# First four F chunks of a SwiGLU kernel with the pieces of D outermost, over eight PSUM banks

## The chip, the cores and the metric

The kernel runs on one core of a Trainium2 chip. Its engines work side by side: TensorE (PE, with its weight loads shown apart as PEld), VectorE (DVE), ScalarE (ACT), GpSimd (POOL) and SyncE (SP). SP and ACT here also issue the DMAs. The metric is the device time of one execution in microseconds (us), taken as the median of several runs. Before the change it is 163.83 us, from three runs between 163.23 and 163.96.

## The reference

The kernel computes a SwiGLU feed-forward layer in bfloat16:

```python
B, S, D, F = 1, 2048, 640, 1536

def reference(x, w_gate, w_up, w_down):
    g = _silu(x @ w_gate)
    u = x @ w_up
    return (g * u) @ w_down
```

## The kernel before

D = 640 is cut in five pieces of 128 rows (`KD`), F = 1536 in twelve chunks of 128 (`KF`), and the 2048 rows of x in four blocks of 512 (`S_BLK`, index `sb`). For a block and a chunk `fc`, `proj` (L189) multiplies the five pieces of one weight chunk into the transposed x and sums them in a PSUM bank: once with w_gate (`pg`), once with w_up (`pu`). `gate` (L204) lets ACT take the Silu of `pg` and DVE multiply it by `pu`; the product goes to `aT`. After twelve chunks, the block is multiplied by w_down (`po_t` at L256 for the last 128 columns, `po_a` at L285 for the first 512) and written out. DVE also computes the last four rows of the input by dot products (L144), a few after each gate of blocks 1 to 3.

Transposed x comes in two ways. Rows 0 to 255 are loaded as they are (`load_x`, one half on SP and one on ACT); TensorE transposes them (`transpose_chunk`, L177), and ACT copies pieces 0 and 1 and DVE pieces 2 to 4 from PSUM into `xT` (L187). All other rows come through transposing DMAs (`turn_x`, L109), rows 256 to 511 by the first of these.

The weights come in chunks of F, given by `W_CHUNKS` (L45). The first, F chunks 0 and 1, comes in four pieces, of which ACT issues pieces 0 to 1 of D of w_gate and 0 to 2 of w_up, and SP the rest (L113 to L116). Then SP issues the transposing load of rows 256 to 511, the later weight chunks in order (`load_w`, L82), and w_down (L122).

`head` (L213) writes out the order of the first stage by hand, and `keep_order` holds TensorE and ACT to it. Eighteen small matmuls on ones (`warm`, L173) run until x is there, then ten transposes, then five more of the small matmuls (`N_GAP`), and then the projections of F chunks 0 and 1: first for rows 0 to 255 (`late` is 256), chunk 0 of w_gate in two halves of 128 rows, and after that for rows 256 to 511, each chunk followed by its gate. The main loop starts at chunk 2 with matmuls 512 columns wide. DVE and SP are held to the order of the program to the end (L308, L309).

PSUM has eight banks here: four under the tag `gu` for `pg` and `pu`, two each under `po_a` and `po_b`, which serve the transposes and later the outputs.

Of the kernel before, what the change touches and what calls it, by code (L numbers as in the profile page):

```python
# [10 lines left out]
def _body(  # L11
# [8 lines left out]
    nc = tc.nc  # L20
    P = nc.NUM_PARTITIONS
    f32 = mybir.dt.float32
# [10 lines left out]
    KD = D // P  # L33
    KF = F // P
    S_BLK = 512
# [1 line left out]
    SUB = S_BLK // P  # L37
    DA = 512
    Q = 32
    N_WARM, N_GAP = 18, 5  # L40
    T = 4
    WT_STEP = 4
    PE_X = 2
    ROW_J = 0
    W_CHUNKS = [(0, 2), (2, 4), (4, 8), (8, 12)]  # L45
    assert D % P == 0 and F % P == 0 and S % S_BLK == 0 and D > DA and SUB == 4

    consts = ctx.enter_context(tc.tile_pool(name="consts", bufs=1))
# [2 lines left out]
    psum = ctx.enter_context(  # L51
        tc.tile_pool(name="psum", bufs=2, space=bass.MemoryType.PSUM)
    )
# [3 lines left out]
    xT = consts.tile([P, KD, S], bf16)  # L57
    wg_sb = consts.tile([P, KD, F], bf16)
    wu_sb = consts.tile([P, KD, F], bf16)
# [14 lines left out]
    wg_v = w_gate.rearrange("(kd p) f -> p kd f", p=P)  # L74
    wu_v = w_up.rearrange("(kd p) f -> p kd f", p=P)
    wd_v = w_down.rearrange("(kf p) d -> p kf d", p=P)

    def wslice(a, b):
        return slice(a * P, b * P)

    def load_w(eng, dst, src, a, b):
        eng.dma_start(out=dst[:, :, wslice(a, b)], in_=src[:, :, wslice(a, b)])  # L82

    def load_x(eng, c0, c1):
        eng.dma_start(out=x_sb[:, c0:c1, :], in_=x_v[:, c0:c1, :])  # L85
# [11 lines left out]
    def keep_order(engine):  # L97

        traced = [i for i in nc.cur_bb.bb.instructions if i.engine == engine]
        for a, b in zip(traced, traced[1:]):  # L100
            issue_order(a, b)
# [5 lines left out]
    def turn_x(c0, c1):  # L107
        s_sl = slice(c0 * P, c1 * P)
        nc.sync.dma_start_transpose(out=xT[:, :, s_sl], in_=xt_v[s_sl])  # L109

    load_x(nc.sync, 0, 1)
    load_x(nc.scalar, 1, 2)
    for dst, src, k in ((wg_sb, wg_v, 2), (wu_sb, wu_v, 3)):  # L113
        for eng, k0, k1 in ((nc.scalar, 0, k), (nc.sync, k, KD)):
            f_sl = wslice(*W_CHUNKS[0])
            eng.dma_start(out=dst[:, k0:k1, f_sl], in_=src[:, k0:k1, f_sl])  # L116
    turn_x(PE_X, SUB)
    nc.scalar.activation(silu_first[:], ones[:, 0:1], ACT.Silu)  # L118
    for a, b in W_CHUNKS[1:]:
        load_w(nc.sync, wg_sb, wg_v, a, b)  # L120
# [5 lines left out]
    def turn_w(dst, src):  # L126
        for a in range(0, KF, WT_STEP):
            nc.sync.dma_start_transpose(
                out=dst[:, a : a + WT_STEP, :], in_=src[:, a : a + WT_STEP, :]
            )  # L130
# [3 lines left out]
        out=x_row[:],  # L134
        in_=x2[S - T : S, :].rearrange("t d -> (t d)").partition_broadcast(P),
# [29 lines left out]
    def do_dots(n):  # L165
        for _ in range(n):
            next(dots, None)
# [3 lines left out]
    def warm(n):  # L171
        for _ in range(n):
            nc.tensor.matmul(  # L173
                pw[:, 0:P], lhsT=ones[:], rhs=ones[:], start=True, stop=True
            )

    def transpose_chunk(c, parts):  # L177
        c_sl = slice(c * P, (c + 1) * P)
        for copy, tag, k0, k1 in parts:
            pt = psum.tile([P, k1 - k0, P], bf16, tag=tag, name="pt")  # L180
            for kd in range(k0, k1):
                nc.tensor.transpose(  # L182
                    out=pt[:, kd - k0, :],
                    in_=x_sb[:, c, kd * P : (kd + 1) * P],
                    identity=ident[:],
                )
            copy(out=xT[:, k0:k1, c_sl], in_=pt[:])  # L187

    def proj(ps, w_sb, fc, sb, c0, c1):  # L189
        for kd in range(KD):  # L190
            nc.tensor.matmul(  # L191
                ps[:, c0:c1],
                lhsT=w_sb[:, kd, fc * P : (fc + 1) * P],
                rhs=xT[:, kd, sb * S_BLK + c0 : sb * S_BLK + c1],
                start=(kd == 0),
                stop=(kd == KD - 1),
            )

    def gu_tiles():
        pg = psum.tile([P, S_BLK], f32, tag="gu", name="pg", bufs=4)  # L200
        pu = psum.tile([P, S_BLK], f32, tag="gu", name="pu", bufs=4)
        return pg, pu

    def gate(pg, pu, sb, fc, n_s):  # L204

        s0 = sb * S_BLK
        sg = work.tile([P, S_BLK], f32, name="sg")
        nc.scalar.activation(sg[:, 0:n_s], pg[:, 0:n_s], ACT.Silu)  # L208
        nc.vector.tensor_tensor(  # L209
            out=aT[:, fc, s0 : s0 + n_s], in0=sg[:, 0:n_s], in1=pu[:, 0:n_s], op=ALU.mult  # L210
        )

    def head():  # L213

        dve, act = nc.vector.tensor_copy, nc.scalar.copy
        split = [(act, "po_a", 0, 2), (dve, "po_b", 2, KD)]  # L220
        late = PE_X * P
        (pg0, pu0), (pg1, pu1) = gu_tiles(), gu_tiles()
        warm(N_WARM)
        transpose_chunk(0, split)
        transpose_chunk(1, split)
        warm(N_GAP)
        proj(pg0, wg_sb, 0, 0, 0, P)
        proj(pg0, wg_sb, 0, 0, P, late)
        proj(pg1, wg_sb, 1, 0, 0, late)
        proj(pu0, wu_sb, 0, 0, 0, late)  # L230
        proj(pu1, wu_sb, 1, 0, 0, late)
        for fc, pg, pu in ((0, pg0, pu0), (1, pg1, pu1)):
            proj(pg, wg_sb, fc, 0, late, S_BLK)
            proj(pu, wu_sb, fc, 0, late, S_BLK)
            gate(pg, pu, 0, fc, S_BLK)
        keep_order(mybir.EngineType.PE)
        keep_order(mybir.EngineType.Activation)

    head()
    for sb in range(NSB):  # L240
        n_s = S_BLK if sb < NSB - 1 else S_BLK - T
        for fc in range(KF):
            if sb == 0 and fc < 2:
                continue
            pg, pu = gu_tiles()
            proj(pg, wg_sb, fc, sb, 0, n_s)
            proj(pu, wu_sb, fc, sb, 0, n_s)
            gate(pg, pu, sb, fc, n_s)
            if sb > 0 and fc < KF - 2:
                do_dots(2)  # L250


        n_t = (SUB if sb < NSB - 1 else SUB - 1) * P
        po_t = psum.tile([P, n_t], f32, tag="po_b", name="po_t")
        for kf in range(KF):
            nc.tensor.matmul(  # L256
                po_t[:],
                lhsT=wd_sb[:, kf, DA:D],
                rhs=aT[:, kf, sb * S_BLK : sb * S_BLK + n_t],
                start=(kf == 0),  # L260
                stop=(kf == KF - 1),
            )
        ot_t = outp.tile([P, n_t], bf16, name="ot_t")
        ot_q = outp.tile([P, n_t], bf16, name="ot_q")
        nc.scalar.copy(ot_t[:], po_t[:])  # L265
        do_dots(3)
        nc.vector.transpose(out=ot_q[:], in_=ot_t[:])  # L267
        for q in range(P // Q):
            nc.scalar.dma_start(
                out=out2[  # L270
                    sb * S_BLK : sb * S_BLK + n_t, DA + q * Q : DA + (q + 1) * Q
                ].rearrange("(i r) c -> r i c", r=Q),
                in_=ot_q[q * Q : (q + 1) * Q, :].rearrange("r (i c) -> r i c", c=Q),
            )

        for j in range(SUB):
            s0 = sb * S_BLK + j * P
            last = sb == NSB - 1 and j == SUB - 1
            cols = [(0, DA, "po_a")]
            if last:  # L280
                cols = [(0, DA // 2, "po_a"), (DA // 2, DA, "po_a"), (DA, D, "po_b")]
            for c0, c1, tag in cols:
                po = psum.tile([P, c1 - c0], f32, tag=tag, name="po_a")
                for kf in range(KF):
                    nc.tensor.matmul(  # L285
                        po[:],
                        lhsT=aT[:, kf, s0 : s0 + P],
                        rhs=wd_sb[:, kf, c0:c1],
                        start=(kf == 0),
                        stop=(kf == KF - 1),  # L290
                    )
                ot = outp.tile([P, c1 - c0], bf16, name="ot" if c1 < D else "ot_b")
                if c1 < D:
                    nc.scalar.copy(ot[:], po[:])  # L294
                    eng = nc.sync
                else:
                    nc.vector.tensor_copy(out=ot[:], in_=po[:])  # L297
                    eng = nc.scalar
                if 0 < j and not last:
                    do_dots(3)  # L300
                if sb == NSB - 1 and j == ROW_J:
                    row_tail()
                eng.dma_start(out=out2[s0 : s0 + P, c0:c1], in_=ot[:])
        if sb == 0:
            turn_x(2 * SUB, 3 * SUB)
            turn_w(wuT, wut_v)
            turn_x(3 * SUB, 4 * SUB)
# [107 lines left out]
```

## Time and profile before

| quantity | value |
|---|---|
| median of three runs | 163.83 us |
| the profiled execution | 163.65 us |
| its span, first to last instruction | 162.3 us |
| PE busy | 159.3 us (98%) |
| DVE busy | 110.9 us (68%) |
| ACT busy | 42.8 us (26%) |
| HBM read, written | 6.88 MB, 2.62 MB |

The profile is one execution. A line such as L191 is a line of the kernel's source, and where a helper holds the instruction, its line. In groups, `out<-in` are the program's names, followed by the shapes and the count; a figure in square brackets is the idle time of the engine before the instruction and what ended it. Matmuls overlap, so the busy times of several in a row are read from their starts. SPq and ACTq are the instruction queues that issue DMAs.

### The profile page before, as it was taken

The numbers are of one execution on the slowest core, as the hardware profiler recorded it, in microseconds if no ns is written. First come the engines' busy times: TensorE is split into PE (matmuls) and PEld (weight loads), VectorE is DVE, ScalarE is ACT, GpSimd is POOL, SyncE is SP. The second block draws the span as 40 slices with busy tenths as digits, with TensorE's granted clock in tenths as the row PEclk, the third lists the DMA queues.
The fourth block names the chain that finished last, engine by engine and source line by source line (L and its number), as shares of the span: only waits on it lengthen the run. The fifth ranks groups of instructions, "written<-read, shape, count | busy, mean of one in ns | idle before, by whom it ended". The sixth has DMA issues, their size and how long they took to land.

```text
span 162.3 us, 2114 instructions
## 1 busy us (share of the span) xinstructions
PE 159.3 (98%) x790; PEld 78.2 (48%) x802; DVE 110.9 (68%) x249; ACT 42.8 (26%) x74; POOL 0.6 (0%) x6
## 2 busy tenths in 40 slices
PE   9999999999999999999999999999999999999995
PEld 8854444444444444444444444444444444445454
DVE  2042233599469999979919999979964999993000
ACT  5032222112222222221222322221214222222121
POOL 1000000000000000000000000000000000000000
PEclk9999999999999999999999999999999999999999
DMA  7999999994179991003110000000320000000312
GB/s 215 261 341 348 362 215 232 226 227 88 43 180 175 227 221 38 4 0 34 65 65 0 4 0 2 0 0 1 64 69 32 0 0 0 0 0 4 50 39 73
DMA packets 42441, 15.86 MB, mean 98 GB/s; under 512 B 33216, under 2 KB 42304, under 8 KB 42432
## 3 DMA queue, kind: packets, MB, share of 16 engines
q1 hardware_dynamic: 33536, 14.72, 37.5%
q10 hardware_dynamic: 8896, 1.02, 4.0%
q8 instruction: 6, 0.10, 0.2%
q14 instruction: 3, 0.02, 0.1%
HBM read 6.88 MB, written 2.62 MB: 59 GB/s over the span
## 4 chain that ended last, share of the span: by engine, by line
PE 96%; DMA 2%; issue 1%; ACTq 0%; DVE 0%
PE pg L191 32%; PE pu L191 32%; PE po_a L285 26%; PE po_t L256 6%; DMA wg_sb<-in_w_gate_dram 2%; ACTq L85 0%; DVE ot_b L297 0%
## 5 line engine op out<-in xcount | busy, mean ns | idle before, releaser
L191 PE MATMUL pg<-xT,wg_sb 128*128 128x512 bf16 (+3 forms) x248 | 59.9, 370 | 0.5
L191 PE MATMUL pu<-xT,wu_sb 128*128 128x512 bf16 (+2 forms) x250 | 59.7, 370 | 0.0
L209 DVE TENSOR_TENSOR aT<-sg,pu 128x512 bf16<-128x512 f32 (+1 forms) x48 | 32.8, 683 | 32.9 <-PE pu L191 28.1
L208 ACT ACTIVATE sg<-pg 128x512 f32<-128x512 f32 (+1 forms) x48 | 28.6, 597 | 71.3 <-PE pg L191 68.1
L285 PE MATMUL po_a<-wd_sb,aT 128*128 128x512 bf16 (+2 forms) x212 | 42.4, 358 | 0.2
L144 DVE SCALAR_TENSOR_TENSOR prod<-wgT,x_row 128x640 f32<-128x640 bf16 x48 | 39.4, 821 | 1.1
L144 DVE SCALAR_TENSOR_TENSOR prod<-wuT,x_row 128x640 f32<-128x640 bf16 x48 | 39.4, 822 | 1.0
L191 PEld LDWEIGHTS <-wg_sb 128*128 128x128 bf16 x255 | 25.0, 100 | 27.3 <-DMA wg_sb<-in_w_gate_dram 0.4
L191 PEld LDWEIGHTS <-wu_sb 128*128 128x128 bf16 x250 | 24.5, 98 | 27.3
L285 PEld LDWEIGHTS <-aT 128*128 128x128 bf16 x216 | 20.7, 98 | 21.6
L294 ACT CAST ot<-po_a 128x512 bf16<-128x512 f32 (+1 forms) x17 | 9.5, 561 | 32.0 <-PE po_a L285 20.9
L256 PE MATMUL po_t<-aT,wd_sb 128*128 128x512 bf16 (+1 forms) x47 | 10.3, 365 | 0.1
L256 PEld LDWEIGHTS <-wd_sb 128*128 128x128 bf16 x48 | 4.7, 98 | 5.1
L297 DVE CAST ot_b<-po_a 128x128 bf16<-128x128 f32 x1 | 0.3, 293 | 9.9 <-PE po_a L285 9.9
L265 ACT CAST ot_t<-po_t 128x512 bf16<-128x512 f32 (+1 forms) x4 | 2.2, 559 | 11.6 <-PE po_t L256 11.6
L144 DVE DVE_READ_ACCUMULATOR prod<-wuT,x_row 128x1 f32 x48 | 4.0, 82 | 0.0
L144 DVE DVE_READ_ACCUMULATOR prod<-wgT,x_row 128x1 f32 x48 | 3.9, 82 | 0.0
L267 DVE STREAM_TRANSPOSE ot_q<-ot_t 128x512 bf16<-128x512 bf16 (+1 forms) x4 | 2.7, 679 | 1.7 <-ACT ot_t L265 1.7
L173 PE MATMUL pw<-ones 128*128 128x128 bf16 x23 | 2.8, 313 | 0.4 <-DVE ones L105 0.4
L187 DVE COPY xT<-pt 128x384 bf16<-128x384 bf16 x2 | 0.7, 358 | 3.1 <-PE pt L182 3.1
L173 PEld LDWEIGHTS <-ones 128*128 128x128 bf16 x23 | 2.4, 147 | 0.4 <-DVE ones L105 0.4
L118 ACT ACT_TABLE_LOAD x1 | 1.3, 1283 | 1.6 <-issue 1.6
(13 smaller groups left out, 4.6 us busy)
## 6 DMA issues: line engine op xcount, KB each, us to landing
wd_sb<-in_w_down_dram SPq DMA_DIRECT2D x1, 1920.0 KB, 14.5
out_dram<-ot SPq DMA_DIRECT2D x15, 128.0 KB, 1.7
wg_sb<-in_w_gate_dram SPq DMA_DIRECT2D x2, 640.0 KB, 7.8
wu_sb<-in_w_up_dram SPq DMA_DIRECT2D x2, 640.0 KB, 8.7
x_row<-in_x_dram SPq DMA_DIRECT2D x1, 640.0 KB, 5.0
out_dram<-ot_q ACTq DMA_DIRECT2D x12, 32.0 KB, 1.9
wg_sb<-in_w_gate_dram SPq DMA_DIRECT2D x1, 320.0 KB, 4.5
wu_sb<-in_w_up_dram SPq DMA_DIRECT2D x1, 320.0 KB, 5.0
```

The source lines that it names most:

```text
L118: nc.scalar.activation(silu_first[:], ones[:, 0:1], ACT.Silu)
L144: nc.vector.scalar_tensor_tensor(out=prod[:], in0=wT[:, fc, :], scalar=1.0, in1=x_row[:, t, :], op0=ALU.mult, op1=ALU.mult, accum_out=acc[ ...
L173: nc.tensor.matmul(pw[:, 0:P], lhsT=ones[:], rhs=ones[:], start=True, stop=True)
L187: copy(out=xT[:, k0:k1, c_sl], in_=pt[:])
L191: nc.tensor.matmul(ps[:, c0:c1], lhsT=w_sb[:, kd, fc * P : (fc + 1) * P], rhs=xT[:, kd, sb * S_BLK + c0 : sb * S_BLK + c1], start=(kd == 0 ...
L208: nc.scalar.activation(sg[:, 0:n_s], pg[:, 0:n_s], ACT.Silu)
L209: nc.vector.tensor_tensor(out=aT[:, fc, s0 : s0 + n_s], in0=sg[:, 0:n_s], in1=pu[:, 0:n_s], op=ALU.mult)
L256: nc.tensor.matmul(po_t[:], lhsT=wd_sb[:, kf, DA:D], rhs=aT[:, kf, sb * S_BLK : sb * S_BLK + n_t], start=(kf == 0), stop=(kf == KF - 1),)
L265: nc.scalar.copy(ot_t[:], po_t[:])
L267: nc.vector.transpose(out=ot_q[:], in_=ot_t[:])
L285: nc.tensor.matmul(po[:], lhsT=aT[:, kf, s0 : s0 + P], rhs=wd_sb[:, kf, c0:c1], start=(kf == 0), stop=(kf == KF - 1),)
L294: nc.scalar.copy(ot[:], po[:])
```

## The change

The first weight chunk now covers F chunks 0 to 3, and SP issues all of it in slices of D: w_gate as piece 0, pieces 1 to 2, pieces 3 to 4, then w_up as pieces 0 to 2 and 3 to 4. The transposing load of rows 256 to 511 is issued after these. For rows 0 to 255, the projections of all four chunks run together, with the piece of D as the outer loop and the chunk as the inner one, first all of w_gate and then all of w_up. Their eight sums stand in eight PSUM banks: `pg` in the four banks of `gu`, `pu` in those of `po_a` and `po_b`. Then rows 256 to 511 follow chunk by chunk, each with its gate, and the main loop starts at chunk 4. Of the five small matmuls ahead of the projections one stays.

```diff
-    N_WARM, N_GAP = 18, 5
+    N_WARM, N_GAP = 18, 1
...
-    W_CHUNKS = [(0, 2), (2, 4), (4, 8), (8, 12)]
+    W_CHUNKS = [(0, 4), (4, 8), (8, 12)]
+    N_EARLY = W_CHUNKS[0][1]
+    WG_KD = [(0, 1), (1, 3), (3, 5)]
+    WU_KD = [(0, 3), (3, 5)]
...
-    for dst, src, k in ((wg_sb, wg_v, 2), (wu_sb, wu_v, 3)):
-        for eng, k0, k1 in ((nc.scalar, 0, k), (nc.sync, k, KD)):
-            f_sl = wslice(*W_CHUNKS[0])
-            eng.dma_start(out=dst[:, k0:k1, f_sl], in_=src[:, k0:k1, f_sl])
+    f_sl = wslice(*W_CHUNKS[0])
+    for dst, src, parts in ((wg_sb, wg_v, WG_KD), (wu_sb, wu_v, WU_KD)):
+        for k0, k1 in parts:
+            nc.sync.dma_start(out=dst[:, k0:k1, f_sl], in_=src[:, k0:k1, f_sl])
     turn_x(PE_X, SUB)
...
-        (pg0, pu0), (pg1, pu1) = gu_tiles(), gu_tiles()
         warm(N_WARM)
         transpose_chunk(0, split)
         transpose_chunk(1, split)
         warm(N_GAP)
-        proj(pg0, wg_sb, 0, 0, 0, P)
-        proj(pg0, wg_sb, 0, 0, P, late)
-        proj(pg1, wg_sb, 1, 0, 0, late)
-        proj(pu0, wu_sb, 0, 0, 0, late)
-        proj(pu1, wu_sb, 1, 0, 0, late)
-        for fc, pg, pu in ((0, pg0, pu0), (1, pg1, pu1)):
-            proj(pg, wg_sb, fc, 0, late, S_BLK)
-            proj(pu, wu_sb, fc, 0, late, S_BLK)
-            gate(pg, pu, 0, fc, S_BLK)
+        pg = [
+            psum.tile([P, S_BLK], f32, tag="gu", name="pg", bufs=4)
+            for _ in range(N_EARLY)
+        ]
+        pu = [
+            psum.tile([P, S_BLK], f32, tag=tag, name="pu")
+            for tag in ("po_a", "po_b", "po_a", "po_b")
+        ]
+        for ps, w_sb in ((pg, wg_sb), (pu, wu_sb)):
+            for kd in range(KD):
+                for fc in range(N_EARLY):
+                    nc.tensor.matmul(
+                        ps[fc][:, 0:late],
+                        lhsT=w_sb[:, kd, wslice(fc, fc + 1)],
+                        rhs=xT[:, kd, 0:late],
+                        start=(kd == 0),
+                        stop=(kd == KD - 1),
+                    )
+        for fc in range(N_EARLY):
+            proj(pg[fc], wg_sb, fc, 0, late, S_BLK)
+            proj(pu[fc], wu_sb, fc, 0, late, S_BLK)
+            gate(pg[fc], pu[fc], 0, fc, S_BLK)
...
-            if sb == 0 and fc < 2:
+            if sb == 0 and fc < N_EARLY:
```

## The prediction

> **What bounds the kernel now.** I read the page first: its busy shares, its clock row and its chain. Columns of the first line are engine, busy us, share of the span and instructions.
>
> ```profile
> PE 159.3 (98%) x790; PEld 78.2 (48%) x802; DVE 110.9 (68%) x249; ACT 42.8 (26%) x74; POOL 0.6 (0%) x6
> ...
> PEclk9999999999999999999999999999999999999999
> ...
> PE 96%; DMA 2%; issue 1%; ACTq 0%; DVE 0%
> ```
>
> TensorE has work for 98% of the span, and 96% of the chain that ended last is TensorE. The 2% of DMA in the chain is one transfer, the first gate weights. From there to the end TensorE hardly stands still, so a microsecond won or lost in the head is one at the end, and nothing after the head needs costing if it is only shifted. The head is read in the timeline (start, length, engine, instruction, count, idle time before and its releaser).
>
> ```profile
> 2.48 0.98 PEld L182 LDWEIGHTS <-x_sb 128*128 128x128 bf16 x10 [0.26 <-DMA x_sb<-in_x_dram]
> 2.48 1.25 PE L182 MATMUL pt<-ident,x_sb 128*128 128x128 bf16 x10
> ...
> 2.96 0.86 ACT L187 COPY xT<-pt 128x256 bf16<-128x256 bf16 x2
> ...
> 3.52 0.74 PE L173 MATMUL pw<-ones 128*128 128x128 bf16 x5
> 3.77 0.36 DVE L187 COPY xT<-pt 128x384 bf16<-128x384 bf16 x1 [0.17 <-PE pt L182]
> ...
> 4.35 1.52 PEld L191 LDWEIGHTS <-wg_sb 128*128 128x128 bf16 x15 [0.36 <-DMA wg_sb<-in_w_gate_dram]
> 4.36 1.80 PE L191 MATMUL pg<-xT,wg_sb 128*128 128x128 bf16 x15
> ...
> 5.99 1.25 PE L191 MATMUL pu<-xT,wu_sb 128*128 128x256 bf16 x10
> ...
> 7.09 0.71 PE L191 MATMUL pg<-xT,wg_sb 128*128 128x256 bf16 x5
> ```
>
> The activations are turned by 4.13 (the DVE copy ends), the weights come at 4.35, and the projections start at 4.36. The other thing to see is the pace. Ten 256-wide matmuls take 5.99 to 7.09, so 109 ns each. The fifteen before take 4.36 to 5.99; five of them are 256 wide (0.55 us), so the ten 128-wide ones cost 1.08 us, 108 ns each: as much as matmuls twice as wide. Is that a floor of the weight load, or a slow clock? The clock row reads full speed all along, so I asked for the weight loads of 128-wide matmuls alone, in the head and in the kernel's last microsecond.
>
> ```profile
> 4.35 1.09 PEld L191 LDWEIGHTS <-wg_sb 128*128 128x128 bf16 x11 [0.36 <-DMA wg_sb<-in_w_gate_dram]
> ```
> ```profile
> 159.54 0.66 PEld L285 LDWEIGHTS <-aT 128*128 128x128 bf16 x11
> ```
>
> Eleven loads take 1.09 us in the head and 0.66 us at the end, about 100 against 56 ns a step. So until about 5.4 us TensorE runs at half pace, whatever the clock row says, and a 256-wide matmul there would take some 213 ns.
>
> **The sum's base.** The profiled execution took 163.65 us (span 162.3 and 1.35 around it), 0.18 below the median 163.83; three runs spread over 0.73.
>
> **First start of the projections.** Removed are ten weight DMAs (four pieces of chunk (0, 2), two on each queue, and six later chunk loads on SP); added are nine, all on SP (five slices of chunk (0, 4), four chunk loads). ACT keeps one of its three. The landings now:
>
> ```profile
> wg_sb<-in_w_gate_dram SPq DMA_DIRECT2D x1, 192.0 KB, 3.6
> wu_sb<-in_w_up_dram ACTq DMA_DIRECT2D x1, 192.0 KB, 4.5
> x_sb<-in_x_dram SPq DMA_DIRECT2D x1, 160.0 KB, 2.4
> x_sb<-in_x_dram ACTq DMA_DIRECT2D x1, 160.0 KB, 2.7
> wg_sb<-in_w_gate_dram ACTq DMA_DIRECT2D x1, 128.0 KB, 3.8
> ```
> ```profile
> 1.00:2.25 1.25, 1.25 (x14) 1.22 (x12) 0.00 (x0) 0.69 (x1) 0.00 (x0) 1.00 0.88 262
> 2.25:3.00 0.75, 0.75 (x9) 0.52 (x7) 0.00 (x0) 0.74 (x3) 0.00 (x0) 1.00 0.96 285
> ...
> 5.00:6.00 1.00, 1.00 (x12) 0.94 (x11) 0.00 (x0) 0.00 (x0) 0.00 (x0) 1.00 1.26 234
> 6.00:8.00 2.00, 2.00 (x21) 1.79 (x19) 0.00 (x0) 0.17 (x1) 0.00 (x0) 1.00 1.20 281
> 8.50:10.50 2.00, 1.95 (x14) 1.27 (x13) 1.34 (x2) 0.60 (x1) 0.00 (x0) 1.00 1.10 342
> ```
>
> (First list: KB, us from issue to landing. Second: stretch, busy us by engine, clock, DMA share, GB/s.) The first slice of w_gate is 128 KB behind 320 KB of x, 459 thousand bytes. At 262 and then 285 GB/s these have moved by 2.7 us. Landing trails movement by 0.6 us for x (328 thousand moved by 2.25, the second half landed at 0.13 + 2.7 = 2.8), by up to 1.0 for w_gate; so the slice lands between 3.3 and 3.7. The start then waits for the turned x instead. The first two pieces of D need ACT's copies alone; these end at 2.96 + 0.86 = 3.82. The last DVE copy starts 0.04 after the last transpose ends (2.48 + 1.25 = 3.73); with twice that, for a signal and a weight load, the start is 3.90. The third piece needs the DVE copy, 4.13, long before its turn. Gain in the start: 4.36 - 3.90 = 0.46 us; the bounds are 0 (slice as late as today) and 0.46 (the copies don't move). I take 0.46, since 3.7 lies below 3.9. The four dropped warm-ups (0.43 us at 107 ns) only filled this wait: the remaining one is through at 3.63, and TensorE stands for 0.27, against 0.30 now (4.06 to 4.36).
>
> **What 0.46 is worth.** In half pace it is 0.46/0.2135 = 2.15 wide matmuls, which at full pace would have cost 2.15 x 0.109 = 0.235 us. So -0.235, if the pace changes at 5.4 as before; the whole -0.46 if it changes before 3.9.
>
> **Merging the ten narrow matmuls of chunk 0** into five wide ones: 10 x 107 = 5 x 213 at half pace, 10 x 56 = 5 x 109 at full pace. Zero either way.
>
> **Chunks 2 and 3 in two halves.** Twenty 512-wide matmuls at 216 ns (1.08 us for five in the chain) become forty at 109: +0.05 us.
>
> **Eight banks, piece of D outermost.** Each matmul now writes another bank than the last. Today that happens every fifth matmul or so, as from pg to pu at 5.99 and back at 7.09, and the pace goes on at 109 ns. I take zero; a gain is excluded, since the pace has no gap to win. The bound above is the 0.07 us that 65 more changes would cost at 1 ns, the reading's grain.
>
> The Trainium skill ("TensorE: Matmul & The Clock Gate", section "A second HAM failure mode: psum-queue depth-cycling") speaks against this step: cycling through PSUM banks made TensorE idle for moments, and its clock fell back. By it the 72 matmuls after 5.4 us could stay at half pace, an estimate of 72 x 0.104 = 7.5 us, which the undisturbed bank changes in these rows don't bear out.
>
> **Will the data keep up on one queue?** Moved bytes go on from 2.7 us at 342 GB/s (1 KB rows on SP alone, the 8.50 row); landing 0.6 to 1.0 later. Wanted: start 3.90, 213 ns each to 5.4, then 109 ns. Slices 1-2 of w_gate: landed 4.1 to 4.5, wanted 4.75. Slices 3-4: 4.8 to 5.2, wanted 5.9. w_up 0-2: 6.0 to 6.4, wanted 6.8. w_up 3-4: 6.8 to 7.2, wanted 8.1. The transposing load of rows 256 to 511 is the step moved most: on SP it stands behind three issues more, of 0.41 to 0.49 us each, so at about 2.9 in place of 1.44, and its bytes stand behind 1.28 MB. At 234 GB/s (5.00 row) it has moved by 7.6 and lands at 8.2 to 8.6; wanted after 40 matmuls at 9.0. Chunk (4, 8) lands by 10.5 and 12.4, wanted 13.4 and 14.5. All covered, thinly for the transposing load. With the slices at 281 GB/s, the row of 512-byte rows, it lands at 8.9 to 9.3. SP's later issues and ACT's table load (1.56, now about 0.6) move ahead or stay; ACT's first copy waits for the transposes anyway.
>
> **PSUM after the head.** Chunk 4 takes the banks of pg 0 and 1, read by ACT some 3 us before; the last, pg 3, is read (0.60 us) 3 us before chunk 5's pu wants it. Four gates follow at 1.09 us each, DVE needs 0.69. Zero.
>
> Sum: 163.65 - 0.235 + 0.05 = 163.47, so 163.5.
>
> **Rivals.**
> 1. Narrow matmuls are bound by their weight loads. Then merging saves 10 x 107 - 5 x 109 = 0.53, the start its whole 0.46: 163.65 - 0.53 - 0.46 + 0.05 = 162.7. The 56 ns loads speak against it.
> 2. The first slice is no earlier (one landing trailed by 1.0 and might by more): 163.65 + 0.05 = 163.7.
> 3. The transposing load, or w_up, comes late. Slowest reading: all of it at 234 GB/s, so the load lands at 9.7 to 10.1 for 9.0; 0.9 of stall: 164.4.
> 4. Slower: half pace lasts longer. TensorE was busy from 0.39 to 5.4 with gaps of 0.2 and 0.3 before the pace changed. With only one warm-up as cover, a slice landing after about 3.9 makes the last gap longer than any seen. If that starts the 5.0 us anew from 3.9, full pace begins at 8.9: 3.5 us at half pace cost 3.5 x 0.49 = 1.7, so 163.47 + 1.7 = 165.2. For it: less cover than today. Against: the expected gap of 0.27 is below the 0.30 that did no harm.
>
> The Trainium skill (same page, section "Part 1: The HAM clock gate (the "warmup" mystery)") puts the change of pace at a free-running window of 3.4 us. That agrees with a change at 5.4 here; by it the moment would differ from run to run, and the sum would lie between 163.24 (change before 3.9) and 163.47.
>
> **How the numbers follow.** Forecast 0.52; rival 1 0.12, 2 0.15, 3 0.13, 4 0.08. The range reaches to rival 1 below and rival 3 above, 162.7 to 164.4, which leaves out rival 4 and little else. Under 0.5% (0.8 us) a measurement can hardly tell from no change, and forecast, 2 and 3 lie within it: faster is rival 1 and 0.05 of the forecast's own spread, 0.17; slower is rival 4 and the tail of 3, 0.11; same 0.72.
>
> **What would show it.** Right: the first pg matmul at about 3.9, its idle time put down to ACT's copy, 213 ns steps and then 109; no wait on w_up or the transposing load; chunk 4 at about 13.4 in place of 13.59, the rest shifted by as much. Wrong: a PE wait on a DMA around 6.8 or 9.0, steps of 213 ns past 5.5, or gate waits at chunk 4.

## The result and the profile after

The changed kernel takes 164.43 us (median of 22 runs, 163.63 to 165.69); the kernel before takes 163.68 in the same comparison (22 runs, 163.13 to 164.11). The ratio is 1.0051, with a 95% interval from 1.0032 to 1.0070: slower by half a per cent, 0.03 us above the predicted range and on the side that was given 0.11. Beside the higher median the spread has grown: five of the 22 runs lie above 165 us, none of before's above 164.2.

The profiled execution of the changed kernel is one of its quicker ones, 163.85 us (span 162.5). Its page:

```profile
PE 159.6 (98%) x813; PEld 79.1 (49%) x813; DVE 110.8 (68%) x249; ACT 42.8 (26%) x74; POOL 0.6 (0%) x6
...
PE 94%; DMA 3%; SPq 1%; DVE 0%; issue 0%
PE pg L194 30%; PE pu L194 30%; PE po_a L300 26%; PE po_t L271 6%; DMA wu_sb<-in_w_up_dram 3%; PE pu L240 1%; SPq L119 1%; SPq L88 0%; DVE ot_b L312 0%
```

For comparison, the last line as the kernel before has it:

```profile
PE pg L191 32%; PE pu L191 32%; PE po_a L285 26%; PE po_t L256 6%; DMA wg_sb<-in_w_gate_dram 2%; ACTq L85 0%; DVE ot_b L297 0%
```

TensorE is as busy as before. But the transfer in the chain is another one: not the first weights of w_gate, which started the projections before, but those of w_up, in their middle. The timeline of TensorE in the head (L240 are the early projections, L194 the rest):

```profile
3.38 0.31 PE L176 MATMUL pw<-ones 128*128 128x128 bf16 x1
3.73 1.01 PE L240 MATMUL pg<-xT,wg_sb 128*128 128x256 bf16 x4
5.14 1.92 PE L240 MATMUL pg<-xT,wg_sb 128*128 128x256 bf16 x16 [0.40 <-DMA wg_sb<-in_w_gate_dram]
7.22 2.36 PE L240 MATMUL pu<-xT,wu_sb 128*128 128x256 bf16 x20 [0.17 <-DMA wu_sb<-in_w_up_dram]
9.42 0.71 PE L194 MATMUL pg<-xT,wg_sb 128*128 128x256 bf16 x5
...
13.79 1.24 PE L194 MATMUL pg<-xT,wg_sb 128*128 128x512 bf16 x5
```

Chunk 4 of the kernel before:

```profile
13.59 1.24 PE L191 MATMUL pg<-xT,wg_sb 128*128 128x512 bf16 x5
```

The projections do start early, at 3.73. After four matmuls TensorE stands until 5.14 for the second slice of w_gate, runs sixteen at full pace, stands again until 7.22 for the first slice of w_up, and reaches chunk 4 at 13.79, where the kernel before is at 13.59. Those 0.2 us are the whole difference between the two profiled executions (163.85 and 163.65); from chunk 4 to the end both take the same.

The landings, as issues with KB and us from issue to landing, and the movement by stretch (last two columns: DMA share, GB/s):

```profile
wg_sb<-in_w_gate_dram SPq DMA_DIRECT2D x1, 128.0 KB, 2.6
wg_sb<-in_w_gate_dram SPq DMA_DIRECT2D x1, 256.0 KB, 4.2
...
wu_sb<-in_w_up_dram SPq DMA_DIRECT2D x1, 384.0 KB, 5.3
```
```profile
3.00:4.00 1.00, 0.97 (x9) 0.74 (x8) 0.72 (x2) 0.52 (x2) 0.00 (x0) 1.00 0.69 190
4.00:5.00 1.00, 0.74 (x4) 0.20 (x2) 0.00 (x0) 0.00 (x0) 0.00 (x0) 1.00 0.91 303
5.00:6.00 1.00, 0.86 (x8) 0.75 (x9) 0.00 (x0) 0.00 (x0) 0.00 (x0) 1.00 1.04 363
...
7.00:8.00 1.00, 0.83 (x9) 0.70 (x8) 0.00 (x0) 0.00 (x0) 0.00 (x0) 1.00 0.73 110
```

The row of the kernel before for 3 to 4 us:

```profile
3.00:4.00 1.00, 1.00 (x12) 1.00 (x10) 0.59 (x2) 0.69 (x3) 0.00 (x0) 1.00 1.07 313
```

From 3 to 4 us the DMA engines moved 190 GB/s where before moved 313, and the first slice of w_up, issued at 1.89, landed at 7.2. The trace has sixteen completion counts for each of these loads, and a load has landed with the last of them. For the second slice of w_gate fifteen came between 3.47 and 4.32 and the last at 5.09; for the first slice of w_up they came between 5.50 and 7.18.

### The profile page after: what moved, and what is told of

Its sections match the earlier page's. It is cut to its first block, busy times and chain, and to the rows that moved or that the text cites. A ratio compares the mean times of both kernels' runs of the same rounds, so it can differ in the third digit from the quotient of the medians.

```text
span 162.5 us, 2147 instructions
## 1 busy us (share of the span) xinstructions
PE 159.6 (98%) x813; PEld 79.1 (49%) x813; DVE 110.8 (68%) x249; ACT 42.8 (26%) x74; POOL 0.6 (0%) x6
## 4 chain that ended last, share of the span: by engine, by line
PE 94%; DMA 3%; SPq 1%; DVE 0%; issue 0%
PE pg L194 30%; PE pu L194 30%; PE po_a L300 26%; PE po_t L271 6%; DMA wu_sb<-in_w_up_dram 3%; PE pu L240 1%; SPq L119 1%; SPq L88 0%; DVE ot_b L312 0%
## 5 line engine op out<-in xcount | busy, mean ns | idle before, releaser
L194 PE MATMUL pg<-xT,wg_sb 128*128 128x512 bf16 (+2 forms) x240 | 57.4, 370 | 0.0
L194 PE MATMUL pu<-xT,wu_sb 128*128 128x512 bf16 (+2 forms) x240 | 57.4, 370 | 0.0
L194 PEld LDWEIGHTS <-wu_sb 128*128 128x128 bf16 x240 | 23.5, 98 | 26.1
L194 PEld LDWEIGHTS <-wg_sb 128*128 128x128 bf16 x240 | 23.5, 98 | 25.9
L240 PE MATMUL pg<-xT,wg_sb 128*128 128x256 bf16 x20 | 2.9, 300 | 0.4 <-DMA wg_sb<-in_w_gate_dram 0.4
L240 PEld LDWEIGHTS <-wg_sb 128*128 128x128 bf16 x20 | 2.0, 106 | 1.4 <-DMA wg_sb<-in_w_gate_dram 0.9
```

The lines of the kernel that those rows point to most:

```text
L194: nc.tensor.matmul(ps[:, c0:c1], lhsT=w_sb[:, kd, fc * P : (fc + 1) * P], rhs=xT[:, kd, sb * S_BLK + c0 : sb * S_BLK + c1], start=(kd == 0 ...
L240: nc.tensor.matmul(ps[fc][:, 0:late], lhsT=w_sb[:, kd, wslice(fc, fc + 1)], rhs=xT[:, kd, 0:late], start=(kd == 0), stop=(kd == KD - 1),)
```

## The experiments

Two theories stood at first. **L**: the slices land late and TensorE stands for them. **P**: with one small matmul in place of five, the gap ahead of the projections keeps TensorE at half pace for longer. All kernels were timed beside the kernel before on the same chip; its medians lay between 163.57 and 163.65. Where a short name is used below, it is that of the run.

### gap5: the small matmuls back

```diff
-    N_WARM, N_GAP = 18, 1
+    N_WARM, N_GAP = 18, 5
```

> The changed kernel with five small matmuls ahead of the projections again in place of one. Theory L (slices of the weights land late on one queue, and TensorE stands for them): the start moves from 3.73 to about 3.85, the wait in the middle shrinks by as much, and the end stays where the changed kernel has it, 164.3 to 164.6 us. Theory P (with one small matmul the gap ahead of the projections keeps the half pace longer): the cover is back, 163.4 to 163.7 us, and the spread falls to that of before.

Measured: 164.31 us (5 runs, 163.82 to 164.36), ratio 1.0036 [1.0023, 1.0049]. The projections start at 3.98, wait twice for w_gate, and the first matmul on w_up starts at 7.19, chunk 4 at 13.75. As L had it: cover ahead of the start changes nothing where the later slices decide.

### before_gap1: the small matmuls taken from the kernel before

```diff
-    N_WARM, N_GAP = 18, 5
+    N_WARM, N_GAP = 18, 1
```

> The kernel before with one small matmul ahead of the projections in place of five, nothing else. L: TensorE stands from 3.6 to 4.36 instead of 4.06 to 4.36 and ends as before, 163.5 to 163.8 us. P: the longer gap keeps the half pace in a part of the runs, 164.2 to 165 us with a wide spread.

Measured: 163.63 us (11 runs, 163.22 to 164.05), ratio 0.9995 [0.9982, 1.0009]. TensorE stood 0.67 us ahead of the projections, and the slowest run took 164.05. P in its first form is wrong: such a gap by itself costs nothing here. (In the profiled run the steps of TensorE fall from 106 to 55 ns at 3.3 us, so there the gap came after the change of pace.)

### twoq: two of the slices on ACT

```diff
-        for k0, k1 in parts:
-            nc.sync.dma_start(out=dst[:, k0:k1, f_sl], in_=src[:, k0:k1, f_sl])
+        for n, (k0, k1) in enumerate(parts):
+            eng = nc.scalar if n % 2 else nc.sync
+            eng.dma_start(out=dst[:, k0:k1, f_sl], in_=src[:, k0:k1, f_sl])
```

> The changed kernel with the second slice of w_gate and the second of w_up issued by ACT, the rest by SP. If L holds and the single queue is what delays the slices: the second slice lands before 4.6, no wait on a DMA after the start, 163.1 to 163.5 us. If L holds and the number of bytes delays them, whatever the queue: waits at the same places, 164.2 to 164.6. P: nothing changes for the gap, 164.4.

Measured: 164.23 us (6 runs, 164.18 to 165.22), ratio 1.0048 [1.0030, 1.0067]. The wait on w_gate is gone, that on w_up is longer:

```profile
4.03 2.93 PE L241 MATMUL pg<-xT,wg_sb 128*128 128x256 bf16 x20
7.93 2.36 PE L241 MATMUL pu<-xT,wu_sb 128*128 128x256 bf16 x20 [0.96 <-DMA wu_sb<-in_w_up_dram]
```

Two queues carried 350 GB/s from 3 to 4 us, and still w_up's first slice landed at 7.9; its second slice, on the other queue, now moved beside it. Spreading the slices over two queues does not take the wait on w_up away.

### narrow and narrow_defer: a quarter of the bytes, and a second limit

```diff
-    f_sl = wslice(*W_CHUNKS[0])
+    f_sl = wslice(0, 1)
...
-    for a, b in W_CHUNKS[1:]:
+    for a, b in [(1, 4)] + W_CHUNKS[1:]:
...
-                        lhsT=w_sb[:, kd, wslice(fc, fc + 1)],
+                        lhsT=w_sb[:, kd, wslice(0, 1)],
```

> The changed kernel with slices one F chunk wide (32 KB a piece of D, a quarter), which the early projections read for all four chunks; chunks 1 to 3 are loaded behind the transposing load. So rows 0 to 255 of chunks 1 to 3 are computed with the weights of chunk 0, and the output is another. Order, banks and small matmuls stay. L: no wait between the start at about 3.75 and the rows from 256 on, the main loop's chunk 4 at 13.0 to 13.4, 163.0 to 163.4 us. P: the gap ahead of the start is still there, 164.4 us and the wide spread.

Measured: 164.39 us (6 runs, 164.10 to 165.03), ratio 1.0050 [1.0035, 1.0065]. Half of L held: from 3.86 the forty early matmuls run without a wait. The gain is gone all the same. A first part is gone in the head: chunk 4 starts at 13.65, no earlier than before. The first twenty matmuls took 3.06 us, so with steps of 213 and 109 ns eight or nine of them ran at half pace, and TensorE waited 0.16 us at 10.75 for the weights of chunk 1, which this kernel loads late. The rest, 0.67 us, is lost later. These are DVE, ACT and TensorE between 33 and 40 us:

```profile
33.37 0.83 DVE L147 SCALAR_TENSOR_TENSOR prod<-wgT,x_row 128x640 f32<-128x640 bf16 x1 [1.50 <-DMA wgT<-in_w_gate_dram]
```
```profile
36.60 2.07 ACTq L284 DMA_DIRECT2D out_dram<-ot_q  x4
38.71 1.07 ACT L309 CAST ot<-po_a 128x512 bf16<-128x512 f32 x2 [4.42 <-DVE prod L147]
```
```profile
39.35 1.02 PE L300 MATMUL po_a<-wd_sb,aT 128*128 128x512 bf16 x4 [0.50 <-ACT ot L309]
```

The transposing load of w_gate for DVE's dot products comes late, DVE waits 1.50 us, three dot products stand ahead of the turn of 128 output columns (the kernel has such dot products in the output stage of every block, the first too, and not only after the gates), ACT issues the four stores of these columns ahead of its first output copy, and TensorE waits for the copy to free a PSUM bank. The stores and the first output copy, in the kernel before and in the changed kernel:

```profile
35.01 1.99 ACTq L269 DMA_DIRECT2D out_dram<-ot_q  x4
37.04 0.59 ACT L294 CAST ot<-po_a 128x512 bf16<-128x512 f32 x1 [2.81 <-DVE prod L144]
```
```profile
35.20 2.86 ACTq L284 DMA_DIRECT2D out_dram<-ot_q  x4
38.11 0.58 ACT L309 CAST ot<-po_a 128x512 bf16<-128x512 f32 x1 [3.68 <-DMA out_dram<-ot_q]
```

Before, that copy ended at 37.63, 1.0 us ahead of TensorE's need (38.62, two tiles of 2.59 us after 33.44). In the profile of the changed kernel it ended at 38.69, 0.13 us ahead of the need at 38.82: there ACT took 2.86 us over the four stores in place of 1.99, and DVE had not waited. So a second limit stands close behind the first (called D from here; what remains lost in the head is H), though in the profile of the changed kernel it cost nothing. Three runs here cut it, by moving the four stores of the first row block behind ACT's second output copy and holding ACT to that order.

```diff
+        def store_t():
...
+        if sb > 0:
+            store_t()
...
                 eng.dma_start(out=out2[s0 : s0 + P, c0:c1], in_=ot[:])
+            if sb == 0 and j == 1:
+                store_t()
...
```

> The kernel with slices of a quarter of the bytes, which the early projections read for all four chunks (so rows 0 to 255 of chunks 1 to 3 are computed with the weights of chunk 0), and with the four stores of the first row block behind the second output copy. With small slices no wait was left in the early projections, but the time stayed at 164.39, with a wait of 0.66 us at 38.5 us for the first output copy. If these are two separate limits: the wait at 38.5 is gone and the time falls to 163.5 to 163.8 us. If the lateness has another cause: 164.2 us or more.

Measured: 164.12 us (11 runs, 163.75 to 164.75), ratio 1.0030 [1.0013, 1.0047]. DVE waits the same 1.5 us for its load, ACT's first copy starts at 36.34 and the wait of TensorE at 38.5 is gone. But this execution waited 0.75 us at 10.2 for the weights of chunk 1. The profiles show the second limit in this kernel. The medians, 0.27 us apart with intervals that overlap, do not price it, and the time lay between the two expectations.

> The changed kernel, with the four stores of the turned 128 output columns of the first row block issued by ACT after its second output copy instead of ahead of the first. Theory H (all that is lost, is lost in the head, to waits on slices): 164.2 to 164.6 us as the changed kernel. Theory D (the head's loads push back the transposing load of w_gate, and through DVE's dot products, the turned columns and ACT's stores the first output copies come too late for TensorE at about 38.5 us): this path is cut, the copies wait for TensorE alone, 163.6 to 164.0 us, and the runs above 165 are gone.

Measured: 164.21 us (6 runs, 163.66 to 164.40), ratio 1.0046 [1.0030, 1.0062], no different from the changed kernel's 1.0051. So in the changed kernel most of the loss is H, as far as these intervals can tell. None of the six runs is above 165; with five of 22 before, that tells little.

> The kernel before with the same move of the four stores. In the profile of before the first output copy ends 1.0 us ahead of TensorE's need, so both H and D expect no difference: 163.5 to 163.8 us.

Measured: 163.59 us (12 runs), ratio 1.0002 [0.9985, 1.0019], as expected.

### gap18: start late

```diff
-    N_WARM, N_GAP = 18, 1
+    N_WARM, N_GAP = 18, 18
```

> The changed kernel with 18 small matmuls ahead of the projections in place of one, so these start some 1.5 us later, near 5.2. H: the waits in the projections are gone but for 0 to 0.3 us ahead of w_up, full pace from the start on, chunk 4 at 13.9 to 14.2, 163.9 to 164.3 us: the early start is worth nothing. D: TensorE reaches the first output copies later by 0.2 to 0.4 us, which hides part of the lateness there; the same times, and a smaller spread.

Measured: 164.22 us (6 runs, 164.06 to 164.66), ratio 1.0049 [1.0032, 1.0067]. In its profile the projections start at 4.86, 1.1 us after those of the changed kernel, and still wait, for slices that landed later in this execution:

```profile
4.86 1.47 PE L240 MATMUL pg<-xT,wg_sb 128*128 128x256 bf16 x12
6.75 1.05 PE L240 MATMUL pg<-xT,wg_sb 128*128 128x256 bf16 x8 [0.42 <-DMA wg_sb<-in_w_gate_dram]
8.00 2.36 PE L240 MATMUL pu<-xT,wu_sb 128*128 128x256 bf16 x20 [0.20 <-DMA wu_sb<-in_w_up_dram]
```

The start is worth nothing. With five profiles of the four-chunk order side by side, the rule of the head can be read off:

| kernel | first start | first w_up matmul | chunk 4 | profiled time |
|---|---|---|---|---|
| after_defer | 3.70 | 7.04 | 13.60 | 163.66 |
| gap5 | 3.98 | 7.19 | 13.75 | 163.82 |
| changed kernel | 3.73 | 7.22 | 13.79 | 163.85 |
| twoq | 4.03 | 7.93 | 14.49 | 164.55 |
| gap18 | 4.86 | 8.00 | 14.56 | 164.62 |

Sixty matmuls of 256 columns lie between the third and the fourth column, 60 x 0.1092 = 6.55 us, and the time is chunk 4 plus 150.06. (Over all sixteen profiles of this document that sum is right to 0.1 us, but for narrow with its 0.67 us at 38 us.) With chunk 4 at 13.59 the kernel before breaks even with a w_up slice used at 7.04. None of the five is earlier. Of the changed kernel's 22 runs, sixteen lie at or below 164.61, where this sum puts a w_up slice used at 8.00, the latest of the five; the other six lie above it.

### two, order2 and two_split_defer: half the bytes

```diff
-    W_CHUNKS = [(0, 4), (4, 8), (8, 12)]
+    W_CHUNKS = [(0, 2), (2, 4), (4, 8), (8, 12)]
```

> The changed kernel with two early F chunks in place of four: slices half as large, chunk (2, 4) loaded later as before. Order with D outermost, one queue, one small matmul stay. If the number of bytes ahead of each step is what makes the slices late (H): start at about 3.8, one wait of at most 0.3 us, main loop two chunks earlier with chunk 4 at 13.2 to 13.5, 163.3 to 163.6 us. If the single queue or the order does it: waits as in the changed kernel, 164 us or more. D: as the bytes ahead of the transposing load of w_gate are the same in number, the copies at 38 us may come late as in the changed kernel, 163.8 to 164.4.

Measured: 164.11 us (7 runs, 163.97 to 164.32), ratio 1.0033 [1.0015, 1.0051]. The first matmul on w_up starts at 5.86, so with fewer bytes ahead of it the slice does land earlier. But there were two waits of about 0.3 us on w_gate, and 0.27 us now goes to the transposing load of rows 256 to 511, which stands behind all slices:

```profile
7.40 0.71 PE L194 MATMUL pg<-xT,wg_sb 128*128 128x256 bf16 x5 [0.27 <-DMA xT<-in_x_dram]
```

Chunk 4 starts at 13.89. H had expected one wait and 163.3 to 163.6 us; the time lies where the single queue or the order was to put it.

> The order alone: D outermost, one small matmul, but two early F chunks and their weights in the pieces, on the queues and in the width of the kernel before. If order and banks cost nothing by themselves: the first piece lands at 4.3 as before, chunk 4 at 13.4 to 13.7, 163.5 to 163.8 us. If changing the bank at every matmul costs, or brings the half pace back: steps over 109 ns after 5.5 us and 164 us or more.

Here the loading code of the kernel before is put back as well. Measured: 163.88 us (12 runs), ratio 1.0027 [1.0004, 1.0050]. The profiled run is the fastest of all, 163.29 us with chunk 4 at 13.19; w_gate's pieces had landed by 4.16 here, by 5.23 in two with the same bytes on one queue. The steps are 109 ns from 4.4 on, but for a wait of 0.2 us for w_up, so another bank at every matmul costs nothing. But the runs fall in two groups: nine from 163.29 to 164.04 and three from 164.90 to 165.10.

> A version meant to be faster: two early F chunks, D outermost, w_gate's slices on SP with the transposing load right behind them, w_up's slices on ACT, the four stores moved as above. If only bytes ahead of a step count: start at 3.9, no wait over 0.2 us, the transposing load landed by 7.0, chunk 4 at 13.1 to 13.5, 163.1 to 163.5 us. If slices land as unevenly as before whatever their size: waits of 0.3 to 0.6 us in the early projections and 163.6 to 164.1 us.

Measured: 163.93 us (12 runs, 163.52 to 165.93), ratio 1.0036 [1.0011, 1.0062]: not faster. In the profile TensorE stands for w_gate's slices twice, by about 0.2 and 0.5 us: slices of D wait for their landings even where they are half as wide.

### oldq and oldq_gap13: the queues of before, and the pace

```diff
-    f_sl = wslice(*W_CHUNKS[0])
-    for dst, src, parts in ((wg_sb, wg_v, WG_KD), (wu_sb, wu_v, WU_KD)):
-        for k0, k1 in parts:
-            nc.sync.dma_start(out=dst[:, k0:k1, f_sl], in_=src[:, k0:k1, f_sl])
+    for dst, src, k in ((wg_sb, wg_v, 2), (wu_sb, wu_v, 3)):
+        for eng, k0, k1 in ((nc.scalar, 0, k), (nc.sync, k, KD)):
+            f_sl = wslice(*W_CHUNKS[0])
+            eng.dma_start(out=dst[:, k0:k1, f_sl], in_=src[:, k0:k1, f_sl])
```

> The changed kernel with the pieces of the first weight chunk cut and issued as in the kernel before (ACT: pieces 0 to 1 of w_gate and 0 to 2 of w_up; SP the rest), still four F chunks wide. In all profiles so far chunk 4 starts 6.55 us after the first piece of w_up has landed (7.0 to 8.0), and the time is 150.05 us more. If the single queue makes that piece late: it lands by 6.5, chunk 4 at 13.0 to 13.3, 163.1 to 163.4 us. If the number of bytes does: it lands at 7.0 to 7.9 again, 164.0 to 164.6 us.

Measured: 165.60 us (4 runs, 165.51 to 166.20), ratio 1.0127 [1.0104, 1.0150], worse than either had it. The first piece, 256 KB, landed at 4.9, w_up's piece at 7.3; that is bytes again. But TensorE came to w_up at 8.89 only:

```profile
4.93 4.12 PE L240 MATMUL pg<-xT,wg_sb 128*128 128x256 bf16 x20 [1.09 <-DMA wg_sb<-in_w_gate_dram]
8.89 2.35 PE L240 MATMUL pu<-xT,wu_sb 128*128 128x256 bf16 x20
```

Twenty matmuls in 3.96 us: with 213 and 109 ns, 17 of them ran at half pace, until 8.6 us. Here half pace does last longer, after a gap of 1.3 us (from the end of the small matmul's step of 0.1 us at 3.52; the profile counts 1.09 us as idle). That is P in a second form, P2: not any gap, but a longer one, puts the change of pace off. Whether the upper groups of order2 and of the changed kernel are of this kind is not shown; in order2's profile the idle time there was 0.33 us, less than the 0.67 of before_gap1.

```diff
-    N_WARM, N_GAP = 18, 1
+    N_WARM, N_GAP = 18, 13
```

> The four-chunk order with the pieces on the queues of before, and 13 small matmuls ahead of the projections in place of one, which end at about 4.9, when the first piece has landed. Without them TensorE stood for 1.3 us, ran the next 17 matmuls at half pace and took 165.60 us. Theory P2 (a long gap in the head puts the change of pace off by some 3 us, and that costs half of it): full pace from about 5 on, the time falls by 1.3 to 1.8 us to 163.8 to 164.3. Theory H alone (only the landing of the pieces counts): 165.3 to 165.8 us as without.

Measured: 164.44 us (12 runs, 163.97 to 168.46; two lie above 165), ratio 1.0049 [1.0030, 1.0068]. The loads are the same; the small matmuls take the place of the gap, and the pace is full from the first projection on:

```profile
3.60 1.59 PE L176 MATMUL pw<-ones 128*128 128x128 bf16 x13
4.99 2.39 PE L240 MATMUL pg<-xT,wg_sb 128*128 128x256 bf16 x20
7.50 2.36 PE L240 MATMUL pu<-xT,wu_sb 128*128 128x256 bf16 x20
```

1.16 us less by twelve matmuls that compute nothing, and all four runs of oldq lie above 165.5: P2 holds for the long gap. And with the pace right, this kernel stands where the changed kernel stands, since w_up is used at 7.50.

> The order alone for two chunks, with six small matmuls ahead of the projections in place of one, which end at about 4.2, when the first piece lands. Without them, nine runs lay between 163.3 and 164.0 and three between 164.9 and 165.1. P2: the upper group is gone, all runs within 163.1 to 164.1, median 163.4 to 163.7. H alone: the upper group stays in about a quarter of the runs.

(order2 with `N_GAP = 6`.) Measured: 163.60 us (12 runs, 163.22 to 164.48), ratio 0.9988 [0.9963, 1.0012]. No run lies near 165, but none of twelve against three of twelve is little evidence. The profile, that of the slowest run, does not show a covered gap either:

```profile
4.92 2.06 PE L240 MATMUL pg<-xT,wg_sb 128*128 128x256 bf16 x10 [0.40 <-DMA wg_sb<-in_w_gate_dram]
6.82 1.25 PE L240 MATMUL pu<-xT,wu_sb 128*128 128x256 bf16 x10
```

The first piece landed later in this execution, TensorE stood 0.40 us, and ten matmuls in 1.90 us means eight of them at half pace, until 6.6. Those eight cost 0.8 us, which is about what this run lies above the median. So P2 is not shown for order2. What the twelve runs do show is that the order with the pieces of D outermost costs nothing against the kernel before and wins nothing. No version here is faster than the kernel before.

## Why the prediction was wrong, step by step

- **What bounds the kernel** was right: TensorE to the end, a head read in shifts. Chunk 4 plus 150.06 us gave the time in the changed kernel's profile and in that of the kernel before. One sentence was too bold, that nothing after the head needs costing if it is only shifted. ACT's first output copies had only 1.0 us to spare before and 0.13 in the changed kernel; in narrow, where the transposing load of w_gate came late, that cost 0.67 us.
- **Start at 3.90**: measured 3.73, since x had landed a little sooner. Right, and worth nothing.
- **The step that failed is the landing of the slices** ("Moved bytes go on from 2.7 us at 342 GB/s ...; landing 0.6 to 1.0 later"). Slices 1 to 2 of w_gate were put at 4.1 to 4.5 and landed at 5.1; w_up's first slice was put at 6.0 to 6.4 and was used between 7.0 and 8.0. Both terms were mis-sized. By the rows of the changed kernel 0.38 + 0.21 + 0.19 + 0.30 + 0.29 MB, the 1.376 MB up to that slice, had moved by 5.8 in place of 5.4, because of the 190 GB/s from 3 to 4 us; and the landing trailed the movement by 1.4 us, not by 1.0 at most, since a load has landed only with the last of its sixteen completion counts and these came 1.6 to 1.7 us apart. The prediction had given these two slices a cover of 0.25 to 0.65 and of 0.4 to 0.8 us; a wait around 6.8 was among its signs of being wrong, and it came just ahead of 7.22. I had taken the row of steady loads at 8.5 us as the rate for the first microseconds, and the slow reading, 234 GB/s, for a rival.
- **"All covered, thinly for the transposing load"** named the wrong victim: in the changed kernel that load was issued at 2.94 and landed at 9.2, and TensorE came to it at 9.42. w_up stood ahead of it with 0.4 us of cover at the late end of its landing.
- **Merging, halves, banks**: right. The steps are 109 ns through sixteen and twenty matmuls, each on another bank than the last, and order2_gap6 prices the whole order at 0.9988. What the prediction weighed against the banks, the Trainium skill's section "A second HAM failure mode: psum-queue depth-cycling" ("TensorE: Matmul & The Clock Gate"), was not borne out here by matmuls 256 columns wide.
- **Rival 3** (the transposing load, or w_up, comes late: 164.4) was the right mechanism, and w_up the right load. That its time is the measured one is luck: the price, a stall of 0.9 us, was worked out for the transposing load, and in the changed kernel's profile the waits on slices cost 0.2 us against before. Its chance of 0.13 was far too low for a step whose cover was below a microsecond.
- **Rival 4** (half pace lasts longer) exists: oldq shows it and oldq_gap13 takes it away. The gap that decides it was put too low, 0.30; by the profiles' idle times, 0.67 did no harm in before_gap1 and 1.09 did in oldq. Whether the five runs of the changed kernel above 165 are of this kind is not settled: no profile caught one. Runs of the same order with five or eighteen small matmuls had none above 164.7 in eleven.
- **The clock** is not the one moment that I took from one profile. By the steps, full pace came between 4.5 and 5.1 in the changed kernel, at 5.5 before, at 3.2 in after_defer, by 4.4 in order2, near 6.4 in before_defer and at 6.6 in order2_gap6. Fifteen of the sixteen profiles lie in this range of 3.4 us; the other is oldq, with 8.6. That agrees with the Trainium skill ("TensorE: Matmul & The Clock Gate", section "Part 1: The HAM clock gate (the "warmup" mystery)"), by which the window is free-running.

The median rose by 0.75 us. By the five profiles the slices take between nothing and 1.0 us, so they can account for it, but only 0.2 us of it is seen in a profile of the changed kernel itself. What the six runs above 164.61 are made of, later slices still, the copies at 38 us or the pace, stays open.

## What to carry to other kernels

An early start is worth only what the next transfers allow: find the last load that the stage needs and count from its landing to the end of the stage. Here sixty matmuls had to follow the first slice of w_up, and pulling four chunks forward put more bytes ahead of it, so the start at 3.7 bought nothing. Price landings in the first microseconds by the rows of those microseconds, not by a later steady rate, count on the last part of a load and not on its bulk, and treat cover of half a microsecond as none.

## What the runs showed that was not expected

- **The last part of a load trails.** In twoq, w_up's slices had moved but for some ten of 640 packets by 7.0 us, and the two slices landed at 7.2 and 7.9. In the changed kernel the movement falls to 110 GB/s from 7 to 8 us, while the transposing load stands behind the slices, against 293 GB/s before. Why one part of a load comes so late was not tried.
- **Small matmuls can be worth more than they cost.** Twelve of them (1.28 us at 107 ns) in a wait of 1.3 us took 1.16 us off the kernel.
- **One queue moved less between 3 and 4 us.** In the seven profiles whose first weights come on SP alone, the DMA engines moved 150 to 263 GB/s in that microsecond; in the nine that use both queues, 285 to 383. For four chunks the last slice of w_gate landed at 4.9 to 5.1 on two queues and at 5.7 to 6.7 on one. In those seven the transposing load is also issued latest, at 2.94 in place of 1.44 to 1.90, so which of the two does it is open. The first slice of w_up gained nothing by it: 7.3 to 7.9 on two queues, 7.0 to 8.0 on one.
- **Landings vary between executions.** The same slices on the same queue landed at 7.0 in after_defer and 8.0 in gap18. A head that is cut to fit one profile will wait in the next.
